# Loads in eight-token rows turned by TensorE, an instruction order from a replay of the queues, and a choice of engine for each step, in an attention-plus-MLP kernel

## The chip, the cores and the metric

The kernel runs on one core of one Trainium2 chip. The metric is the device time of one execution in microseconds (us); lower is better. Each execution also has a span, from the first to the last instruction that the profiler counts; in this case the time is 1.7 to 1.9 us longer than the span in every execution. Engines are named as in the profile: PE is TensorE (matmuls), PEld its weight loads, DVE VectorE, ACT ScalarE, POOL GpSimd, SP SyncE.

## The reference

A recurrent attention over 4 batches x 8 heads x 768 tokens x 48 channels, and then a two-layer MLP on the 3072 tokens:

```python
for t in range(S):                       # per batch and head, state is 48 x 48
    cur = outer(u * k[t], v[t])
    y[t] = r[t] @ (state + cur)
    state = w[:, None] * state + outer(k[t], v[t])
x = y with heads side by side            # (3072, 384)
h = x @ w_in                             # 384 -> 2048
g = maximum(0.01 * h, h)
out = g @ w_out                          # 2048 -> 384, fp32
```

## The kernel before

Both kernels cut the 3072 tokens into 24 stages of 128 tokens (six per batch). A stage goes through: load r, k, v; scale r and k by powers of w out of tables (`kq`); transpose (`kt`); scores (PE), causal mask (`at`, DVE); y (PE) plus the bonus term `bv`; a state update (PE, `s`); transpose of y into `xT`; first layer (PE, eviction, leaky ReLU into the ring `gring`); second layer (PE), eviction `o`, store. Every one of these is recorded as an operation of a plan, a list scheduler simulates the engines and fixes the order of each engine's instructions, and the program is emitted in that order. An engine thus waits for its next instruction in the fixed order, even where a later one could run.

Loads are issued per stage, one row of 48 fp32 (192 B) per token and head, 1024 rows in each load:

```python
def go_rk():
    ins = []
    for xi, src in enumerate((r, k)):
        a = src[b].rearrange("h t d -> t h d")[c * L:c * L + L, :, :]
        ins.append(SP.dma_start(vr.t[:, xi, :, :], a))
    return ins
# ... order of the first loads and weight pieces; "@k" style gates make one wait for another's landing
DMA_SEQ = "st0 wc st1 u wi0@rk0 wi1@rk0 st2@v1 wo0@rk2 st3@v2 wo1@v2 st4@rk3"
```

Each step belongs to one engine. The leaky ReLU is ScalarE's: it evicts the PSUM bank once as it is, and in some groups a second time with the factor 0.01 (otherwise DVE multiplies in SBUF); DVE takes the maximum:

```python
e1 = op("ACT", 0.52, (lambda ev=ev: ev(False)), ..., reads=[bk], writes=[gv...])
if two:
    hparts.append(op("ACT", 0.52, (lambda ev=ev: ev(True)), ..., reads=[bk], writes=[hv]))
# ...
m = op("DVE", 1.22 if nu == 4 else 0.69, V.tensor_tensor(..., ALU.max), ...)
```

The second number of `op` is the duration that the scheduler reckons with; in `schedule` a transfer starts when the one before is through (`x0 = max(o.end + 0.6, dma_free)`) and lands 1.4 us after its last byte.

Of the kernel before, what the change touches and what calls it, by code (L numbers as in the profile page):

```python
# [24 lines left out]
GROUPS = [1, 1] + [2] * 11  # L25
NRAW, NKQ, NKT, NVB, NAT, NPU, NB, NBV, NY, NOUT, NSS, NG = 5, 3, 3, 5, 2, 2, 3, 3, 3, 4, 2, 16
NBANK = 5
NH = 3
OB_DVE = 20
TWO = [1, 1, 1, 1] + [1, 1, 0, 0] * 4 + [0, 0, 0, 0]  # L30
MOE_BANKS = 3
QKT_DMA_FROM = 8
YT_DMA_FROM = 99
LEAD = 3.0
PERIOD = 6.0
WARM_UNTIL = 14.0
WI, WO = [4, 12], [8, 8]
DMA_SEQ = "st0 wc st1 u wi0@rk0 wi1@rk0 st2@v1 wo0@rk2 st3@v2 wo1@v2 st4@rk3"
BONUS_DVE = 0
BONUS_PE = 2  # L40
MASK_SPLIT = 2
XT_DVE = 0
S_ACT = 0
KT_SPLIT = 2
CROSS = 0.07
SAME = 0.06


class Op:
    __slots__ = ("eng", "dur", "fn", "deps", "prio", "name", "vals", "new", "xfer", "sem",  # L50
                 "start", "end", "done", "pos", "ndma", "left", "users", "snap", "mark", "waits", "semval", "slots", "count", "behind")

    def __init__(self, eng, dur, fn, name, prio):
        self.eng, self.dur, self.fn, self.name, self.prio = eng, dur, fn, name, prio
        self.deps, self.vals, self.new = set(), [], []
        self.xfer, self.sem, self.ndma = None, None, 1
        self.start = self.end = self.done = None
        self.users = []
        self.mark = False
        self.count = 1  # L60


class Val:
    __slots__ = ("pool", "name", "writers", "readers", "slot", "prev")

    def __init__(self, pool, name):
        self.pool, self.name = pool, name
        self.writers, self.readers = [], []
        self.slot = None
        self.prev = ()  # L70
# [6 lines left out]
class Pool:  # L77
    def __init__(self, name, bufs):
        self.name, self.bufs = name, bufs
        self.cur = [None] * len(bufs)  # L80
        self.until = [0.0] * len(bufs)


class Plan:

    def __init__(self):
        self.ops = []

    def op(self, eng, dur, fn, name, prio, reads=(), writes=(), after=(), xfer=None, sem=None, ndma=1,
           behind=(), joins=()):  # L90
        o = Op(eng, dur, fn, name, prio)
        o.xfer, o.sem, o.ndma = xfer, sem, ndma
        for v in reads:
            assert v.writers, (name, v.name)
            for p in v.writers:
                o.deps.add(p)
            v.readers.append(o)
        for v in writes:
            if v.writers:
                for p in v.writers:  # L100
                    o.deps.add(p)
            else:
                o.new.append(v)
            v.writers.append(o)
        for p in after:
            o.deps.add(p)
        o.deps.discard(o)
        o.behind = set(behind)
        for v in joins:
            o.behind.add(v.writers[0])  # L110
            v.writers.append(o)
            o.vals.append(v)
        self.ops.append(o)
        return o

    def schedule(self, filler=None, filler_dep=None, filler_until=0.0):
        engs = ["PE", "DVE", "ACT", "POOL", "SP"]
        free = {e: 0.8 for e in engs}
        dma_free = 0.0
        for o in self.ops:  # L120
            o.left = len(o.deps | o.behind)
            for d in o.deps | o.behind:
                d.users.append(o)
        cand = {e: [o for o in self.ops if o.eng == e and o.left == 0] for e in engs}
        order = {e: [] for e in engs}
        moe_open = 0
        ndone = 0

        def slot_for(v):
            best = None  # L130
            p = v.pool
            for i, c in enumerate(p.cur):
                if c is None:
                    t, dd = p.until[i], ()
                else:
                    us = c.readers + c.writers
                    if any(u.start is None for u in us):
                        continue
                    t, dd = max(u.done for u in us), us
                if best is None or t < best[0]:  # L140
                    best = (t, i, dd)
            return best

        def lat(d, o):
            if d.xfer is not None:
                return d.done
            if d.eng == o.eng:
                return d.end if d.eng == "PE" else d.end + SAME
            return d.end + CROSS

        while ndone < len(self.ops):
            pick = None
            for e in engs:
                best = None
                for o in cand[e]:
                    if o.name[0] == "moe" and o.new and o.name[1] >= MOE_BANKS:
                        pass
                    st = free[e]
                    for d in o.deps:
                        x = lat(d, o)  # L160
                        if x > st:
                            st = x
                    for v in o.vals:
                        for d in v.prev:
                            st = max(st, lat(d, o))
                    ok = True
                    sl = []
                    for v in o.new:
                        if v.pool is None:
                            continue  # L170
                        if getattr(v.pool, "limit", None) is not None and v.name[0] == "m":
                            open_m = sum(1 for c in v.pool.cur if c is not None and c.name[0] == "m"
                                         and any(u.start is None for u in c.readers + c.writers))
                            if open_m >= v.pool.limit:
                                ok = False
                                break
                        b = slot_for(v)
                        if b is None:
                            ok = False
                            break  # L180
                        sl.append((v, b))
                        if b[0] + CROSS > st:
                            st = b[0] + CROSS
                    if not ok:
                        continue
                    key = (max(st, free[e] + 0.02), o.prio)
                    if best is None or key < best[0]:
                        best = (key, o, st, sl)
                if best is None:
                    continue  # L190
                if pick is None or best[2] < pick[2]:
                    pick = best
            assert pick is not None, ("stuck", {e: [(o.name) for o in cand[e]][:8] for e in engs})
            _, o, st, sl = pick
            e = o.eng
            if e == "PE" and filler is not None and st < filler_until + 10:
                free[e] = max(free[e], filler_dep.end + CROSS)
                while free[e] < filler_until:
                    fd = 0.22 if free[e] < 6.8 else 0.11
# [3 lines left out]
                    f.start = free[e]  # L203
                    f.end = f.done = free[e] + fd
# [4 lines left out]
            o.start, o.end = st, st + o.dur  # L209
            o.done = o.end  # L210
            free[e] = o.end
            if o.xfer is not None:
                x0 = max(o.end + 0.6, dma_free)
                dma_free = x0 + o.xfer
                o.done = dma_free + 1.4
            o.slots = []
            for v, (t, i, dd) in sl:
                for u in dd:
                    o.deps.add(u)
                v.slot = i  # L220
                v.pool.cur[i] = v
                v.prev = tuple(dd)
# [3 lines left out]
            cand[e].remove(o)  # L226
            for u in o.users:
                u.left -= 1
                if u.left == 0:
                    cand[u.eng].append(u)  # L230
            ndone += 1
        return order

    def sync(self, order):
        for e, lst in order.items():
# [4 lines left out]
        for e, lst in order.items():  # L240
            for o in lst:
                if o.xfer is not None:
                    cnt[o.sem] = cnt.get(o.sem, 0) + 16 * o.ndma
                    o.semval = cnt[o.sem]
        known = {e: {} for e in order}
        for o in seq:
            e = o.eng
            kn = known[e]
            need = {}
            for d in o.deps:  # L250
                if d.xfer is not None:
                    key, val = ("D", d.sem), d.semval
                else:
                    if d.eng == e and e == "PE":
                        continue
                    key, val = ("E", d.eng), d.pos
                if kn.get(key, -1) >= val:
                    continue
                if key not in need or need[key][0] < val:
                    need[key] = (val, d)  # L260
            keep = []
            items = sorted(need.items(), key=lambda kv: -kv[1][1].done)
            for key, (val, d) in items:
                if kn.get(key, -1) >= val:
                    continue
                keep.append(d)
                d.mark = True
                kn[key] = max(kn.get(key, -1), val)
# [3 lines left out]
            o.waits = keep  # L272
            o.snap = dict(kn)
        for e, lst in order.items():
# [609 lines left out]
```

## Time and profile before

| kernel before | value |
|---|---|
| time, 3 runs | 197.82 us median (197.74 to 199.0) |
| profiled execution | 200.67 us, span 198.9 us |
| mean granted TensorE clock in it | 0.949 |

The page's first part gives, for each engine, busy us (share of the span) and the number of instructions:

```profile
PE 175.0 (88%) x1753; PEld 127.3 (64%) x1753; DVE 133.3 (67%) x179; ACT 116.0 (58%) x226; POOL 83.5 (42%) x82
```

The costliest groups (line, engine, operation, output<-inputs, shapes, count | busy us, mean ns | idle time of the engine just before them, and what ended it):

```profile
L636 PE MATMUL ps_g<-xT,win 128*128 128x256 bf16 (+1 forms) x624 | 75.9, 274 | 1.3 <-ACT xT L616 1.3
L711 PE MATMUL ps_g<-wout,gring 128*128 128x384 bf16 x384 | 68.5, 331 | 3.5 <-DVE gring L691 3.2
```

L636 and L711 are the two dense layers, 144 us of PE's 175. The list of waits (who waited for what: us in total, times, longest) shows the hole of the head as PE and DVE saw it:

```profile
PE ps_g L484 <- DVE kq L457: 9.6, 2, 7.9
...
DVE kq L457 <- DMA raw<-in_k_dram: 7.9, 1, 7.9
```

One wait of 7.9 us of DVE for a k load (the second line) became one wait of 7.9 us of PE for DVE (the longest of the first).

### The profile page before, as it was taken

To read this page: it belongs to the slowest core of one execution; us is meant where nothing else is said; L and a number is where in the kernel's file an instruction comes from. 1 tells how busy PE (TensorE), PEld (TensorE's weight loads), DVE (VectorE), ACT (ScalarE), POOL (GpSimd) and SP (SyncE) were. 2 spreads that over 40 slices of the span, in tenths; PEclk is the share of its full clock that TensorE was granted. 3 is DMA by queue.
4 is the path that set the end of the run, shared out by engine and by line. 5 is a ranking of instruction groups with operands and counts; after the bars stand their busy time and mean duration, and the time that the engine had idled before them with its cause. 6 is when DMAs were issued, how large, how long until landed. Compare 5 with 4: busy or idle time off the path is not lost.

```text
span 198.9 us, 4292 instructions
## 1 busy us (share of the span) xinstructions
PE 175.0 (88%) x1753; PEld 127.3 (64%) x1753; DVE 133.3 (67%) x179; ACT 116.0 (58%) x226; POOL 83.5 (42%) x82
## 2 busy tenths in 40 slices
PE   7640989488998998999998999999999999999983
PEld 5430779245865765776866757667677676676751
DVE  2521605876999999899796784975975538364531
ACT  3800648413985794657794657946679555346430
POOL 2310350435699999967867455541331100000000
PEclk9995557879999999999999999999999999999999
DMA  5799699699998589998999867982334220110112
GB/s 110 110 205 208 122 140 184 115 215 243 212 202 164 134 168 179 223 175 170 241 179 227 166 135 166 146 167 82 53 92 96 52 79 3 39 45 0 42 40 81
DMA packets 99253, 26.91 MB, mean 135 GB/s; under 512 B 93088, under 2 KB 98848, under 8 KB 99232
## 3 DMA queue, kind: packets, MB, share of 16 engines
q1 hardware_dynamic: 92896, 18.75, 52.3%
q0 software_dynamic: 2880, 3.15, 9.6%
q10 hardware_dynamic: 3456, 4.72, 6.8%
q8 instruction: 14, 0.23, 0.5%
q14 instruction: 7, 0.06, 0.1%
HBM read 20.84 MB, written 4.72 MB: 128 GB/s over the span
## 4 chain that ended last, share of the span: by engine, by line
PE 58%; DVE 22%; ACT 7%; DMA 6%; SPq 3%; issue 2%; ACTq 0%; DVEq 0%
PE ps_g L711 26%; PE ps_g L636 22%; DVE gring L691 7%; DMA raw<-in_k_dram 6%; ACT gring L669 4%; DVE kq L457 4%; DVE at L552 3%; PE ps_xy L535 3%; DVE y L575 2%; PE ps_g L613 2%; PE ps_g L484 1%; PE ps_g L568 1%; ACT h L668 1%; PE ps_g L564 1%; DVE h L687 1%
## 5 line engine op out<-in xcount | busy, mean ns | idle before, releaser
L636 PE MATMUL ps_g<-xT,win 128*128 128x256 bf16 (+1 forms) x624 | 75.9, 274 | 1.3 <-ACT xT L616 1.3
L711 PE MATMUL ps_g<-wout,gring 128*128 128x384 bf16 x384 | 68.5, 331 | 3.5 <-DVE gring L691 3.2
L669 ACT ACTIVATE gring<-ps_g 128x512 bf16<-128x512 f32 x96 | 57.8, 606 | 21.9 <-PE ps_g L636 15.4
L636 PEld LDWEIGHTS ps_g<-xT,win 128*128 128x128 bf16 x624 | 56.8, 103 | 9.1 <-ACT xT L616 2.1
L711 PEld LDWEIGHTS ps_g<-wout,gring 128*128 128x128 bf16 x384 | 36.4, 99 | 28.6 <-DVE gring L691 5.6
L523 POOL TENSOR_TENSOR bv<-vb,b 128x384 bf16<-128x384 bf16 x22 | 25.0, 1135 | 46.2 <-DVE y L575 28.8
L691 DVE TENSOR_TENSOR gring<-gring,h 128x2048 bf16<-128x2048 bf16 (+1 forms) x26 | 32.5, 1253 | 11.0 <-ACT h L668 9.4
L552 DVE TENSOR_TENSOR at<-ps_xy,tri 128x1024 bf16<-128x1024 f32 x22 | 26.8, 1217 | 15.6 <-PE ps_xy L535 15.6
L457 DVE TENSOR_TENSOR kq<-raw,tab 128x768 bf16<-128x768 f32 x24 | 27.0, 1127 | 12.3 <-DMA raw<-in_k_dram 7.9
L467 POOL TENSOR_TENSOR pu<-raw,ubc 128x384 f32<-128x384 f32 x22 | 26.5, 1205 | 8.0 <-DMA raw<-in_k_dram 8.0
L668 ACT ACTIVATE h<-ps_g 128x512 bf16<-128x512 f32 x48 | 28.6, 614 | 1.1 <-PE ps_g L636 0.9
L469 POOL TENSOR_TENSOR pr<-pu,raw 128x384 f32<-128x384 f32 x22 | 27.2, 1235 | 1.3
L722 ACT ACTIVATE o<-ps_g 128x384 f32<-128x384 f32 x22 | 10.8, 490 | 25.9 <-PE ps_g L711 25.9
L461 ACT ACTIVATE vb<-raw 128x384 bf16<-128x384 f32 x24 | 12.8, 534 | 16.2 <-DMA raw<-in_v_dram 9.8
L616 ACT ACTIVATE xT<-ps_g 128x384 bf16<-128x384 bf16 x24 | 12.0, 498 | 9.0 <-PE ps_g L613 8.8
L687 DVE TENSOR_SCALAR h<-gring 128x2048 bf16<-128x2048 bf16 x12 | 9.1, 757 | 10.3 <-ACT gring L669 10.3
L575 DVE TENSOR_TENSOR y<-ps_g,bv 128x384 bf16<-128x384 f32 x24 | 13.2, 551 | 1.6 <-PE ps_g L568 1.4
L484 PE MATMUL ps_g<-idn,kq 128*128 128x128 bf16 x64 | 5.3, 231 | 9.6 <-DVE kq L457 9.6
L471 DVE TENSOR_REDUCE b<-pr 128x8 f32<-128x384 f32 x22 | 11.9, 541 | 2.6 <-POOL pr L469 1.4
L484 PEld LDWEIGHTS ps_g<-idn,kq 128*128 128x128 bf16 x64 | 4.2, 103 | 10.3 <-DVE kq L457 10.2
L535 PE MATMUL ps_xy<-kt 48*128 48x128 bf16 x192 | 9.7, 222 | 1.1 <-DVE kt L491 0.8
L613 PE MATMUL ps_g<-idn,y 128*128 128x128 bf16 x72 | 8.5, 231 | 2.4 <-DVE y L575 2.4
(51 smaller groups left out, 104.3 us busy)
## 6 DMA issues: line engine op xcount, KB each, us to landing
raw<-in_r_dram SPq DMA_DIRECT2D x24, 192.0 KB, 3.6
raw<-in_k_dram SPq DMA_DIRECT2D x24, 192.0 KB, 3.8
raw<-in_v_dram SPq DMA_DIRECT2D x24, 192.0 KB, 3.9
out_dram<-o ACTq DMA_DIRECT2D x24, 192.0 KB, 1.9
wout<-in_moe_w_out_dram POOLq DMA_DIRECT2D x2, 768.0 KB, 11.1
win<-in_moe_w_in_dram POOLq DMA_DIRECT2D x1, 1152.0 KB, 11.4
win<-in_moe_w_in_dram POOLq DMA_DIRECT2D x1, 384.0 KB, 6.0
kt<-kq SPq DMA_TRANSPOSE x16, 3.5
```

What stands on the lines that cost most here:

```text
L457: o = op("DVE", 0.96, lambda: V.tensor_tensor(kq.t[:, :, 0:D], vr.t[:, 0:2, :, :].rearrange("p a h d -> p (a h) d"), tab[l][:, :, :, :].re ...
L467: op(bn, bd_, lambda: be.tensor_tensor(pu.t[:, :, :], vr.t[:, 1, :, :], ubc[:, :, :], ALU.mult), f"pu{n}", pr_a(n, 0.2), reads=[vr, f_u], ...
L469: op(bn, bd_, lambda: be.tensor_tensor(pr.t[:, :, :], pu.t[:, :, :], vr.t[:, 0, :, :], ALU.mult), f"pr{n}", pr_a(n, 0.3), reads=[vr, pu], ...
L523: op("POOL", 0.95, lambda: G.tensor_tensor(bv.t[:, :].rearrange("p (h d) -> p h d", d=D), vb.t[:, :].rearrange("p (h d) -> p h d", d=D), b ...
L535: o = PE.matmul(xy.t[:, 512 * s + 128 * i:512 * s + 128 * i + 128], kt.t[rows, HP + i, :], kt.t[rows, i, :], start=(i == 0), stop=True, sk ...
L552: op("DVE", 1.23, lambda: V.tensor_tensor(at.t[:, :, :], xy.t[:, :].rearrange("p (h t) -> p h t", t=128), tri[:, :].unsqueeze(1).to_broadc ...
L575: op("DVE", 0.57, lambda: V.tensor_tensor(ys.t[:, :], y.t[:, 0:DM], bv.t[:, :], ALU.add), f"ys{n}", pr_a(n, 0.5), reads=[y, bv], writes=[ys])
L636: o = PE.matmul(bk.t[:, 128 * T * f:128 * T * (f + 1)], win[:, s, 128 * fb:128 * fb + 128], xT[:, s, L * n0:L * n0 + L * T], start=(s == 0 ...
L668: return A.activation(o_ap, i_ap, AF.Copy, scale=LRELU_SLOPE)
L669: return A.activation(o_ap, i_ap, AF.Copy)
L691: (lambda j0=j0, j=j, hv=hv, flat=flat: V.tensor_tensor(flat(dst(j0, j + 1)), flat(dst(j0, j + 1)), flat(hdst(hv, 0, nu)), ALU.max)),
L711: o = PE.matmul(bk.t[:, 0:DM], gring[:, n % NG, fb, :], wout[:, fb, :], start=(fb == 0), stop=(fb == NFB - 1))
```

## The change

The intent is to feed PE earlier and to keep it fed. Its parts:

1. **Wide rows.** r and k of the first six stages and v of the first five are loaded as 128 rows of 1536 B (eight tokens of one head), so that one transfer has 128 rows in place of 1024. The tokens then lie along the row, and PE turns them with 16 small matmuls against columns of the identity.
2. **y turned by DMA** from stage 10 on, in place of PE transposes and evictions.
3. **Alternatives.** An operation may name a second and third engine with its duration there, and the scheduler takes whichever lets it start first.
4. **Replay.** After scheduling, the order is replayed against a model of the DMA queues. The landing times that come out are used for a second and a third plan, and the best of the three is kept.
5. **Sizes.** Weight pieces 4, 4, 8 each, a new order of the first loads with gates, single-stage groups at both ends, the last tile's second layer in three column thirds, four banks for the MLP, a `gring` of 12 stages instead of 16.

The diff, cut to its core:

```diff
-GROUPS = [1, 1] + [2] * 11
+GROUPS = [1, 1, 1, 1, 2, 2, 2, 2, 2, 2, 2, 2, 2, 1, 1]
-MOE_BANKS = 3
-QKT_DMA_FROM = 8
-YT_DMA_FROM = 99
-LEAD = 3.0
+MOE_BANKS = 4
+QKT_DMA_FROM = 9
+YT_DMA_FROM = 10
+LEAD = 5.5
-WARM_UNTIL = 14.0
-WI, WO = [4, 12], [8, 8]
-DMA_SEQ = "st0 wc st1 u wi0@rk0 wi1@rk0 st2@v1 wo0@rk2 st3@v2 wo1@v2 st4@rk3"
+WARM_UNTIL = 20.0
+WI = [4, 4, 8]
+WO = [4, 4, 8]
+DMA_SEQ = 'st0 st1 wi0@k1 wi1@wi0 st2@k0 uw@v0 w@r0 st3@v0 wi2@v3 u@r0 wo0@v2 wo1@v0 wo2 st4@v0 st5@v0 st6@v4'
+NWIDE = 6
+V_WIDE = 5
+GS_POOL = 8
+LAST_SPLIT = 3
+PASSES = 3
...
+                wide = n < NWIDE and (xi < 2 or n < V_WIDE)
+                    if wide:
+                        a = dram(src, (b * H * S + c * L) * D, [[8 * D, 16], [S * D, H], [1, 8 * D]])
+                        return [SP.dma_start(vr.t[:, xi, :, :].rearrange("p h d -> p (h d)"), a)]
...
+        def turn(ps, part):
+            for j in range(8):
+                for s in range(2):
+                    o = PE.matmul(ps[64 * s:64 * s + D, 64 * j:64 * j + 64], part(j), idn[:, s:128:2],
+                                  start=(j == 0), stop=True, skip_group_check=True)
...
+            elif kind == "uw":           # w and u as 4 rows, 1.5 KB together, turned by PE at once
+                def go_wu():
+                    return [A.dma_start(wu[:, 0, :, 0:D], dram(w, 0, [[2 * D, HP], [D, 2], [1, D]])),
+                            A.dma_start(wu[:, 1, :, 0:D], dram(u, 0, [[2 * D, HP], [D, 2], [1, D]]))]
+                op("ACT", 1.55, go_wu, "wu", -186, writes=[f_wu], after=gates, ...)
...
+                parts.append(op("ACT", 0.6, (lambda ev=ev: ev("ACT")), f"ga_{n0}_{j}", pr + 0.05, reads=[bk],
+                                alt=("DVE", 0.69, ...) if n0 >= GA_ALT else None, **kw))
...
+                    op("DVE", 0.79 if nu == 4 else 0.46, (lambda sc=sc: sc("DVE")), f"gs_{n0}_{j}", pr + 0.07,
+                       after=parts[-nu:], writes=[hv],
+                       alt=[("ACT", 1.92 if nu == 4 else 1.06, ...)]
+                       + ([("POOL", 2.6 if nu == 4 else 1.4, ...)] if n0 < GS_POOL else []))
...
+    landing, best = {}, None
+    for _ in range(PASSES):
+        P, order = build(landing)
+        landing, made = P.execute(order)
+        made += sum(P.execute(order, case)[1] for case in CASES)
+        made /= 1 + len(CASES)
+        if best is None or made < best[0]:
+            best = (made, P, order)
```

## The prediction

> **What bounds the kernel now.** I read the page first, then the chain of waits in order of time, then busy time by windows, then the groups by line. The busy tenths, in 40 slices of 5 us each:
>
> ```profile
> PE   7640989488998998999998999999999999999983
> DVE  2521605876999999899796784975975538364531
> PEclk9995557879999999999999999999999999999999
> DMA  5799699699998589998999867982334220110112
> ```
>
> The reader is to see two regimes. From about 50 us on, TensorE (PE) is busy nine tenths or more at full clock: there the kernel is bound by the matmuls of the two dense layers. Before that, PE has holes, and its clock is at half in slices 4 to 6. The windows (core, PE busy, PEld, DVE, ACT, POOL, granted clock, DMA share, GB/s) put the hole in place:
>
> ```profile
> 12.00:14.00 2.00, 0.02 (x1) 0.00 (x0) 0.00 (x0) 0.00 (x0) 0.00 (x0) 1.00 1.09 208
> 16.00:18.00 2.00, 0.00 (x0) 0.00 (x0) 0.00 (x0) 0.00 (x0) 0.00 (x0) 0.50 1.06 202
> 28.00:30.00 2.00, 2.00 (x22) 2.00 (x20) 0.00 (x0) 1.80 (x4) 0.00 (x0) 0.50 1.27 184
> 36.00:38.00 2.00, 1.20 (x16) 0.68 (x16) 2.00 (x4) 0.00 (x0) 1.21 (x1) 1.00 0.94 169
> 60.00:80.00 20.00, 17.85 (x187) 12.74 (x187) 19.86 (x24) 13.39 (x28) 19.59 (x16) 1.00 0.78 160
> ```
>
> From 12 to 18 us no engine works and DMA is full: everything waits for data. At 28 us PE is busy but at half clock. At 36 us VectorE (DVE) has no idle time while PE has; from 60 to 80 us DVE is busy 19.86 of 20 us. The chain says which data:
>
> ```profile
> 6.97 11.94 DMA raw<-in_k_dram
> 18.93 0.97 DVE kq L457
> ...
> 26.23 6.90 PE ps_g L636 x72
> ...
> 195.99 0.56 DVE o L722
> ```
>
> The k rows of the second stage took 11.94 us to land, behind both pieces of the first weight matrix. DVE stands in program order before that data, so even the first stage's output waits until 19.81 us. Dense work starts in earnest at 26.23 us.
>
> So the span of 198.9 us is a sum: 26.2 us of head, 169.7 us from there to PE's last matmul at 195.97, 2.9 us of last eviction and store. In the middle part, slow clock from 26.2 to 31.5 and from 39.5 to 42 us costs (5.3 + 2.5)/2 = 3.9 us, idle PE some 8.7 us (summed from the windows), and the rest, about 157 us, is matmul work.
>
> **What the Trainium skill says.**
> "TensorE: Matmul & The Clock Gate", section "Why this matters for your kernels": avoid PE gaps over about 3 us between bursts, or the clock falls back to half. The trace agrees: PE stops near 12 us, the clock averages 0.72 in 14:16 and 0.50 in 16:18. It also shows 0.70 in 38:40 after four microseconds in which PE was about half busy with no gap that long.
> "DMA: Bandwidth & Descriptors", section "Specifications": transfers need at least 512 B to reach line rate. The trace agrees: q1, nearly all 192-byte rows, holds the 16 engines 52.3% of the span for 92,896 packets, 0.523 x 198.9 x 16 / 92,896 = 17.9 ns each, 10.7 B/ns; the output's q10 (3456 packets, 4.72 MB, 6.8%) takes 62.6 ns for 1365 B, 21.8 B/ns.
> "SBUF — State Buffer", in its list of what contends: a DVE instruction with two SBUF inputs excludes a GpSimd one that reads SBUF. The trace fits: kq takes 941 ns at least and 1751 at most, GpSimd's pr 993 to 1859.
>
> **The change part by part.**
>
> *Wide rows.* Seventeen loads (r, k of six stages, v of five) become 128 rows of 1536 B instead of 1024 of 192 B. DMA time of one: before 64 packets per engine x 17.9 = 1.15 us; after 8 x 62.6 = 0.50 us. Over 17 that is 11 us of full-rate DMA off the head, and the first weight piece is held until the second stage's k has landed. SP issues a load in 0.4 to 0.6 us, so that k is issued by about 3.5 us and lands near 6 (a load takes 3.6 to 3.8 us unloaded before). The hole from 11 to 19.8 us goes. Price: turning. Each of 17 tiles needs 16 small matmuls; eight of 48 columns took 0.20 us warm (25 ns each), so I take 28 ns: 7.6 us. Eleven turns back of four transposes at 0.056 (eight took 0.45): 2.5 us. The old transposes of stages 0 to 5 go: 6 x 0.45 = 2.7 us. Each turn also needs an eviction of 0.6 to 0.7 us on DVE or ScalarE.
>
> *y turned by DMA from stage 10 on.* 14 sets of three PE transposes go (14 x 0.27 = 3.8 us of PE), and 14 evictions of 0.50 on ScalarE.
>
> *Engines per step.* Counting the built orders and multiplying by the group means: DVE goes from 133 us to about 146, as it takes 15 of the 96 first evictions (0.69 each, 10.4), 9 output copies, and fewer scalings; ScalarE goes from 116 to roughly 115 to 125, since the second eviction with a factor (48 x 0.61 = 29) becomes a scaling out of SBUF. Neither exceeds PE.
>
> *Groups and the last tile.* Single-stage groups at both ends, and the last tile in thirds. Before, the tail shows 0.50 us of PE wait before the last 2.77 us, then 2.9 us. Thirds shorten the last copy from 0.56 to about 0.25; 48 matmuls of 128 columns at 0.057 cost 2.7 against 2.6. A gain of about 0.3 us.
>
> PE sum before, warm: dense 24 x (4 x 0.66 + 2.60) = 125.8; scores 24 x 0.33 = 7.9; y 24 x 0.20 + 20 x 0.25 = 9.8; states 6.3; y turns 24 x 0.27 = 6.5; transposes 8 x 0.45 = 3.6; total 159.9. After: 125.8 + 7.9 + 9.8 + 6.3 + 10 x 0.27 + 3 x 0.45 + 7.6 + 2.5 + 0.5 = 164.5. **PE gets 4.6 us more work, not less**; the gain is that work starts earlier.
>
> Where in time? In the built order of the changed kernel PE has done about 25 us of this before its first matmul of the second layer, and 139.6 us remain (all but 10 of 96 first-layer groups, all second-layer ones, stages 6 to 23). When does it reach that point? DVE must by then have done 31.7 us by group means less 2.3 us of constants that wait for no data; the means overstate by 7% (same count for the whole kernel before: 143 against 133 busy), so 27.5 us, starting near 3.5 us: not before 31 us. In a chain of PE turn, eviction, mask, product, DVE will not be full; at 85% it is 36 us. A second estimate by DMA: the weights held 16 engines 9.6% of the span, 19.1 us; six stages wide 17 x 0.50 + 1.15 = 9.7; tables 1 to 2; a start near 3 us: all weights in by 34 us if DMA never rests, and the gated queue will rest some. **I take 36 us** for that point.
>
> From there: 139.6 x 1.01 = 141 us (the same counting on the kernel before, from its first long second-layer block at 39.5 us, gives 147.8 of work, and 147.8 + 1.2 cold + 5.7 idle falls 1.8 us short of 195.97, hence 1%). Idle: before it was 4.0 us from 60 to 196; DVE is now more loaded (about 102 us beside PE's 112 until attention ends), the replayed order and a fourth bank work against that; I take 4 us. End 2.7. Sum 36 + 141 + 4 + 2.7 = 183.7 of span; the median is 197.82 where this span is 198.9, factor 0.995: 182.7, say **183 us**.
>
> **The rivals.**
> *DVE becomes the bound.* For: 146 us of work in 183, full from 60 to 80 us already before; a PE bank held by a late eviction stops PE. Against: the last attention is spread later in the new order. It would cost 4 to 8 us more: 187 to 191.
> *Weights late or PE cold.* The weights now follow each other through gates on one queue; if the last piece lands near 42 instead of 36 us, or if a half-busy PE loses its clock between 8 and 30 us as it did at 39 us, the dense part starts 3 to 6 us later: 186 to 189.
> *The gain is smaller because the hole was hidden.* If the middle were bound by DVE or DMA rates rather than by when PE starts, an earlier start would only become idle time later: 190 or more, within 2% above 193.9. Against: from 80 to 180 us PE is over 95% busy at full clock, so a shift of the start shifts the end.
> *Better than thought.* Replay leaves PE idle under 2 us after 33 us: 178.
>
> **Range and chances.** The sum's loose terms are the 36 us point (32 to 42) and idle (2 to 8); together 177.5 to 190. Slower than 2% would need all of the 15 us eaten: 1%. Within 2% needs two rivals at once: 5%. Faster by over 2%: 94%.
>
> **What would show it.** In the changed profile: no window under 20 us without work; the second stage's k landed by 7 us; first-layer matmuls from 16 to 20 us; the first second-layer matmul at 34 to 40 us; clock 1.0 after 15 us; PE from then to its end at 95% or more, for 141 us plus idle; DVE busy 142 to 150 us; the last eviction near 0.25 us. It is wrong if the first second-layer matmul comes after 43 us, if PE idles over 8 us after it, or if PE's clock shows 0.5 in several slices.

## The result

| kernel | times of the executions, us | median | clock of the executions |
|---|---|---|---|
| before | 199.0, 197.82, 197.74, 199.0 | 198.41 | 0.949 in the profiled one |
| changed | 185.95, 186.94, 186.91, 186.15 | 186.53 | 0.981, 0.982, 0.972, 0.981 |

The ratio is 0.940, with a 95% interval of 0.935 to 0.945. It is the mean time of one kernel's fast runs over the mean of the other's fast runs in the same rounds, so it is not quite the ratio of the medians. The profiled execution of the changed kernel is the one of 185.95 us, span 184.2 us. First its page, by engine, then the busy tenths in 40 slices (of 4.6 us each now):

```profile
PE 173.1 (94%) x2108; PEld 135.1 (73%) x2108; DVE 150.2 (82%) x218; ACT 113.6 (62%) x186; POOL 88.3 (48%) x89
...
PE   7749998979999999899999999999999999999994
DVE  4956799885699995997799967996995978787792
PEclk9995799999999999999999999999999999999999
DMA  4899799999870099694979999939999732120202
```

PE has almost as many busy us as before (173.1 against 175.0) in a shorter span. DVE has 17 us more. The row of PEclk has one dip left, of two slices, where it had five slices below 0.8. The windows that answer to those shown of before (us, then PE, PEld, DVE, ACT and POOL busy, granted clock, DMA share, GB/s):

```profile
12.00:14.00 2.00, 0.00 (x0) 0.00 (x0) 0.00 (x0) 0.00 (x0) 1.89 (x2) 0.88 1.17 271
14.00:16.00 2.00, 1.74 (x24) 1.47 (x25) 1.01 (x5) 0.00 (x0) 0.00 (x0) 0.50 1.06 257
16.00:18.00 2.00, 2.00 (x24) 1.75 (x22) 1.61 (x2) 1.29 (x5) 0.00 (x0) 0.50 1.09 289
28.00:30.00 2.00, 2.00 (x55) 1.85 (x56) 2.00 (x2) 1.79 (x6) 1.32 (x2) 1.00 1.12 207
36.00:38.00 2.00, 1.71 (x34) 1.50 (x34) 0.51 (x2) 1.99 (x5) 1.98 (x2) 1.00 1.08 203
60.00:80.00 20.00, 19.23 (x192) 14.58 (x190) 17.79 (x22) 16.95 (x26) 15.70 (x12) 1.00 0.75 140
```

Two things are to be seen. From 60 to 80 us PE is now busy 19.23 of 20 us (before 17.85) and DVE has room. From 12 to 14 us PE, DVE and ACT stand still again, and the clock is at half for the 6 us that follow. A third thing needs a longer window: from 22 to 36 us DVE has no idle time at all (13.96 of 14 us busy), while PE is busy 13.26. The list of waits says what ended that stop, and the chain of waits (start us, us, what) carries it to the dense part:

```profile
PE ps_g L591 <- DMA wu<-in_u_dram: 3.0, 1, 3.0
```

```profile
8.04 6.17 DMA wu<-in_u_dram
...
34.83 2.79 POOL h L1035
...
38.93 1.22 DVE at L908
...
177.84 3.99 PE ps_g L1069 x56
181.85 0.29 DVE o L1081
```

The new stop is a wait for two loads of 1.5 KB each (the comment in the code counts them as one): the rows of w and of u that PE turns into columns. The plan gates them behind the first stage's v. The load of u is issued at 8.04 us and lands 6.17 us later, and PE stands before it in its fixed order. The window from the first matmul of the second layer's first block to PE's last (span us, PE busy, clock, DMA share, GB/s):

```profile
40.74:181.85 141.11, 140.16 (x1470) 1.00 0.67 138
```

In these 141.1 us PE is idle for less than 1 us. The kernel before, from its first long second-layer block at 39.50 us to its last matmul at 195.97, took 156.5 us, of which 150.8 were busy and 5.6 idle. So the 14.7 us of span split as follows: 10.7 us less PE time after the point where the dense part begins, 4.7 us less idle time after it, 0.6 us less tail, minus 1.2 us because that point comes later, at 40.7 instead of 39.5.

### The profile page after: what moved, and what is told of

It is laid out like the page before. It is cut to its first block, busy times and chain, and to the rows that moved or that the text cites. A ratio compares the mean times of both kernels' runs of the same rounds, so it can differ in the third digit from the quotient of the medians.

```text
span 184.2 us, 5027 instructions
## 1 busy us (share of the span) xinstructions
PE 173.1 (94%) x2108; PEld 135.1 (73%) x2108; DVE 150.2 (82%) x218; ACT 113.6 (62%) x186; POOL 88.3 (48%) x89
## 4 chain that ended last, share of the span: by engine, by line
PE 58%; POOL 13%; ACT 8%; DVE 7%; issue 7%; DMA 5%; ACTq 0%; POOLq 0%
PE ps_g L1007 24%; PE ps_g L1069 23%; POOL pu L872 5%; POOL bv L878 4%; DMA wu<-in_u_dram 3%; POOL pr L874 3%; PE ps_xy L890 3%; DVE at L908 3%; ACT h L1036 2%; ACT gring L1021 2%; PE ps_g L920 2%; PE ps_g L924 2%; DMA lnp<-in_w_dram 2%; POOL h L1035 2%; DVE gring L1042 1%
## 5 line engine op out<-in xcount | busy, mean ns | idle before, releaser
L1069 PE MATMUL ps_g<-wout,gring 128*128 128x384 bf16 (+1 forms) x416 | 69.9, 314 | 0.0
L1007 PEld LDWEIGHTS ps_g<-xT,win 128*128 128x128 bf16 x720 | 63.0, 114 | 4.3 <-issue 1.0
L1021 ACT ACTIVATE gring<-ps_g 128x512 bf16<-128x512 f32 x81 | 45.8, 600 | 19.5 <-PE ps_g L1007 18.7
L1042 DVE TENSOR_TENSOR gring<-gring,h 128x2048 bf16<-128x2048 bf16 (+1 forms) x30 | 34.3, 1147 | 8.2 <-ACT h L1036 6.6
L1036 ACT ACTIVATE h<-gring 128x2048 bf16<-128x2048 bf16 (+1 forms) x21 | 32.3, 1545 | 9.9 <-DVE gring L1021 9.4
L878 POOL TENSOR_TENSOR bv<-vb,b 128x384 bf16<-128x384 bf16 x18 | 19.5, 1088 | 34.4 <-DVE b L876 31.1
L1021 DVE CAST gring<-ps_g 128x512 bf16<-128x512 f32 x15 | 10.1, 692 | 1.9 <-PE ps_g L1007 1.6
L1081 DVE COPY o<-ps_g 128x384 f32<-128x384 f32 (+1 forms) x12 | 5.8, 486 | 4.8 <-PE ps_g L1069 4.8
L890 PEld LDWEIGHTS ps_xy<-kt 48*128 48x128 bf16 x192 | 5.5, 95 | 5.2 <-issue 2.8
L924 PE MATMUL ps_g<-vb,at 128*128 128x48 bf16 x192 | 9.0, 186 | 0.0
L920 PE MATMUL ps_g<-s,kt 128*128 128x96 bf16 x80 | 6.9, 211 | 1.9 <-DVE at L908 1.7
```

Of the source, the lines that this page charges most:

```text
L878: op("POOL", 1.1, lambda: G.tensor_tensor(bv.t[:, :].rearrange("p (h d) -> p h d", d=D), vb.t[:, :].rearrange("p (h d) -> p h d", d=D), bb ...
L890: o = PE.matmul(xy.t[:, 512 * s + 128 * i:512 * s + 128 * i + 128], kt.t[rows, HP + i, :], kt.t[rows, i, :], start=(i == 0), stop=True, sk ...
L1007: o = PE.matmul(bk.t[:, 128 * T * f:128 * T * (f + 1)], w_in_block(s, j * per + f), xT[:, s, L * n0:L * n0 + L * T], start=(s == 0), stop= ...
L1021: return A.activation(o_ap, i_ap, AF.Copy) if e == "ACT" else V.tensor_copy(o_ap, i_ap)
L1036: return A.activation(o_ap, i_ap, AF.Copy, scale=LRELU_SLOPE)
L1042: return V.tensor_tensor(flat(dst(j0, j + 1)), flat(dst(j0, j + 1)), h_ap, ALU.max)
```

## The experiments

All runs gave the correct result. The kernel before was run beside them, between 197.5 and 201.9 us. "The first second-layer matmul" is dated from the chain or from that line's instructions; "the dense part" is the time from there to PE's last matmul. Experiments that change constants let the planner make a new order, so they change more than the one thing; those marked "order kept" edit the finished order and change nothing else.

### The changed kernel again

No edit. It tells how much executions of one program differ, and serves beside the others.

> The changed kernel once more, unedited, as the measure for the others of this call: 185.5 to 187.5 us, and the same hole in the profile: TensorE idle from about 12 to 14.3 us for the small load of w and u columns, half clock from there to about 20 us, first second-layer matmul near 40.7 us.

Measured: 182.88, 185.7, 186.08 and 187.35 us at clocks 0.991, 0.991, 0.972 and 0.972. A run over 1.5% above the fastest of its kernel counts as slow, so three of these carry that label and no ratio is given; with all eight executions of this kernel the mean is 186.0 us (185.5 for these four alone). In the profiled one (182.88) the small load landed at about 11.7 us instead of 14.2, and the stop is shorter:

```profile
PE ps_g L591 <- DMA wu<-in_u_dram: 1.3, 1, 1.3
```

Its first second-layer matmul comes at 37.5 us and its last matmul ends at 178.77: again 141.3 us. The same program, 3.2 us earlier at the start of the dense part and 3.1 us shorter in span. So the head alone sets the difference, and the head differs with the landing of one small load and with the clock.

### The small load early (order kept)

```diff
     _, P, order = best
+    wu_op = [o for o in order["ACT"] if o.name == "wu"][0]
+    wu_op.deps = {d for d in wu_op.deps if d.pk is None}      # no gate
+    wu_op.start = max(d.start for d in wu_op.deps) + 0.001
+    order["ACT"].remove(wu_op)
+    order["ACT"].insert(1, wu_op)                             # second on its queue
```

> Only the place of the two small loads of w and u columns changes: issued second on ScalarE's queue, without the gate; every other engine's order is the same. Theory (the point of the first second-layer matmul came 4.7 us late because of this load: 2.25 us of stop, then some 6 us at half clock, then the second weight piece issued behind work that waits for it): no stop at 12 us, no half clock from 14 to 20, first second-layer matmul at 36 to 38 us, time 182 to 183.5 us. Rival A (VectorE sets the head: busy 18.15 of 20 us between 20 and 40): first second-layer matmul only 1 to 2 us earlier, time 185 to 186. Rival B (the last weight piece, landing near 41 us, sets it): the first second-layer matmul comes earlier but TensorE then waits before the matmuls that need the last piece, time 184.5 to 186.

Measured: 183.04, 185.11, 185.38, 184.31 us, median 184.71, ratio to before 0.931 (0.923 to 0.938). Windows of this kernel:

```profile
12.00:14.00 2.00, 2.00 (x39) 1.34 (x36) 2.00 (x6) 1.25 (x5) 2.00 (x2) 1.00 1.18 278
14.00:16.00 2.00, 1.55 (x47) 1.22 (x46) 1.83 (x4) 2.00 (x8) 1.71 (x3) 1.00 1.02 278
```

and the end of its head and of its chain:

```profile
31.94 2.79 POOL h L1035
...
37.85 0.65 PE ps_g L1069 x4
...
174.93 4.00 PE ps_g L1069 x56
178.95 0.29 DVE o L1081
```

The stop is gone and PE is busy from 12 to 14 us at full clock. The dense part starts at 37.85 instead of 40.74 us and lasts 141.1 us, to the tenth what it lasted in the changed kernel. So against the first profile of the changed kernel the small load and the half clock after it cost 2.9 us. Against its repeat they cost nothing: there PE waited 1.3 us for the load and the dense part still began at 37.5 us. Where PE waited 4.2 and 4.4 us (the profiles of the last tile whole and of y turned by PE, with the same gate) it began at 42.05 and 42.51 us. In the means the gain is less than the theory had: 1.0 us against the four executions of the same rounds (184.46 against 185.5), 1.5 against all eight, and the two sets overlap. The load lands at a different time in every profiled execution with this gate (11.7, 14.2, 15.4 and 15.7 us), and three of these four executions still have two or three half-clock windows (stretches of some 3.4 us at half clock, counted from the span and the mean clock as in the last section); that this is why the mean gains less is likely, but the unprofiled executions don't show it.

### y turned by PE throughout

```diff
-YT_DMA_FROM = 10
+YT_DMA_FROM = 99
```

> Turning of y kept on TensorE in all stages; order replanned. Theory (after about 41 us TensorE's work alone sets the end): 14 sets of 0.27 us come back, 3.8 us, time 189 to 191 us. Rival (TensorE has slack, VectorE or ScalarE bound): within 1 us of the changed kernel, or more than 6 us slower through ScalarE's 14 evictions.

Measured: 191.55, 189.02, 189.61, 190.09 us, median 189.85, ratio 0.959 (0.951 to 0.967).

```profile
42.51 0.65 PE ps_g L1069 x4
...
184.39 2.87 PE ps_g L1069 x48
```

```profile
PE ps_g L1069 <- DVE gring L1042: 1.4, 1, 1.4
```

The dense part takes 187.26 - 42.51 = 144.75 us, some 3.7 us more than 141.1. Fourteen sets of transposes at 0.27 us would be 3.8 us, but the agreement is in part chance: in that window PE is busy 142.21 us, only 2.05 more than the 140.16 of the changed kernel, and idle 1.6 us more. Of the idle time 1.4 us is one wait for the leaky ReLU before the last block, which the changed kernel doesn't have. So more PE work lengthens that part, but not one for one as I had it; whether the wait comes from the transposes or only from the new order isn't shown. (The 1.8 us by which the profiled execution starts later is its small load, for which PE waited 4.4 us.)

### Narrow loads

```diff
-DMA_SEQ = 'st0 st1 wi0@k1 wi1@wi0 st2@k0 uw@v0 w@r0 st3@v0 wi2@v3 u@r0 wo0@v2 wo1@v0 wo2 st4@v0 st5@v0 st6@v4'
-NWIDE = 6
+DMA_SEQ = 'w st0 uw@v0 st1 wi0@k1 wi1@wi0 st2@k0 st3@v0 wi2@v3 u@r0 wo0@v2 wo1@v0 wo2 st4@v0 st5@v0 st6@v4'
+NWIDE = 0
```

> Wide rows undone (no stage loaded in eight-token rows, w's table first in the queue), all else of the change kept. Theory (the gain comes from an earlier dense part that the wide rows allow): most of the gain is lost, first second-layer matmul back to 45 us or later in terms of work left, time 192 to 198 us although TensorE has about 7 us less to do. Rival (the new order and engine choice carry the gain, the rows do not matter): 184 to 189 us.

Measured: 197.48, 197.82, 196.79, 198.4 us, ratio 0.998 (0.990 to 1.005): the whole gain is gone. From its waits and its chain:

```profile
ACT vb L810 <- DMA raw<-in_v_dram: 12.3, 3, 10.0
...
PE ps_st L943 <- ACT vb L810: 10.0, 1, 10.0
```

```profile
18.12 19.80 DMA raw<-in_v_dram
...
46.13 0.65 PE ps_g L1069 x4
```

One narrow load of 192 KB, beside the weight pieces, took 19.80 us to land and held PE for 10 us. The Trainium skill, "DMA: Bandwidth & Descriptors", section "Queues, rings and completion order", says that each DMA engine takes turns between the queue rows it has work for, a packet at a time. A load of 1024 small pieces beside large weight rows would then need several turns on each engine. The two long landings fit that picture (19.80 us here and 11.94 us in the kernel before, against medians of 3.6 to 3.9 us), but no run counts the turns, so this cause is argued and not shown.

### Narrow loads in another order

```diff
-DMA_SEQ = 'st0 st1 wi0@k1 wi1@wi0 st2@k0 uw@v0 w@r0 st3@v0 wi2@v3 u@r0 wo0@v2 wo1@v0 wo2 st4@v0 st5@v0 st6@v4'
-NWIDE = 6
+DMA_SEQ = 'w st0 uw@r0 st1 u wi0@k0 wi1@k0 wi2@k0 st2@v1 wo0@k2 wo1@k2 wo2@k2 st3@v2 st4@k3'
+NWIDE = 0
```

> Narrow rows again as in e4, but the loads of stages and weights ordered as in the kernel before, so that the weights do not stand in front of stages 3 and 4 as they did in e4 (a load there took 19.8 us). Theory (narrow rows cannot be fed beside the weights whatever the order; the wide rows carry the gain): first second-layer matmul at 43 us or later, time 191 to 198. Rival (e4 only showed a bad order of loads; narrow rows with a fit order keep most of the gain): 185 to 190.

Measured: 197.23 and 198.75 us, ratio 0.999 (0.989 to 1.009). Here the weights come early and the first second-layer matmul is at 26.8 us, and it does not help:

```profile
60.00:80.00 20.00, 17.13 (x177) 13.11 (x178) 19.80 (x23) 10.25 (x19) 19.86 (x13) 0.91 0.49 106
80.00:100.00 20.00, 16.49 (x176) 13.13 (x174) 15.86 (x19) 12.14 (x20) 19.63 (x13) 1.00 0.73 156
```

PE starves from 60 to 100 us, while DVE and then POOL are full; its longest waits there are 3.5 us for the leaky ReLU and 2.1 us for y, both from DVE. So the date of the first matmul alone does not predict the time. That too little attention had been done by then is my reading, which no run tests. Both narrow kernels lose the whole gain, but the constants were tuned for wide rows, so the 11 to 12 us are an upper figure for what wide rows are worth, not a measurement of it.

### The last tile whole

```diff
-LAST_SPLIT = 3
+LAST_SPLIT = 1
```

> The last tile in one piece again, nothing else moved. One look: the part from the last first-layer matmul to the end of the span, which does not depend on the head. In the changed kernel the last 56 second-layer matmuls take 3.99 us and the span ends 2.4 us later. Theory: the last block takes 3.9 us and the span ends 2.7 us after it, so 0.2 to 0.3 us more in all. Rival: nothing, or a gain, because 48 narrow matmuls cost what the shorter last copy saves.

One execution, 187.76 us (state unknown, span 186.0), so only its end is read:

```profile
179.15 3.91 PE ps_g L1069 x24
183.09 0.56 DVE o L1081
```

From the start of that last block to the end of the span: 186.0 - 179.15 = 6.85 us, against 184.2 - 177.84 = 6.36 us in thirds. The thirds save some 0.5 us. The copy shrinks by 0.27 us (0.56 to 0.29), as predicted; what follows it, the last store, is 0.3 us shorter, and the narrower matmuls give 0.1 us back (3.99 for 3.91). The expectation had 0.2 to 0.3 us.

### One engine for each step

```diff
-        if alt is not None:
+        if False:
             o.alts.extend(alt if isinstance(alt, list) else [alt])
```

> The choice between engines undone: each step keeps its first engine (all turned tiles evicted by VectorE, all scalings on VectorE, all output copies and first evictions on ScalarE), order replanned. Theory: VectorE then has about 21 x 1.5 us of scalings less what they cost there (0.76 against 1.9), some 16 us more work, minus 10.4 us of first evictions, near its limit already; the head gets 12 evictions more on VectorE and starts later, TensorE waits in the middle: 189 to 195 us. Rival (engines per step hardly matter while TensorE is the bound): 186 to 188.

Measured: 197.56, 195.66, 191.74, 196.35 us; three are over 1.5% above the fastest, so no ratio is given. The one execution labelled fast, 191.74 us, is 5.7 us above the mean of the changed kernel (186.0), on another chip. The profiled execution is a slow one (197.56, clock 0.991). It shows this:

```profile
40.00:60.00 20.00, 16.39 (x226) 12.41 (x222) 19.97 (x31) 9.15 (x18) 7.61 (x8) 1.00 0.53 108
```

DVE is full (19.97 of 20 us) while ACT and POOL are under half, and PE is busy 16.39. Over the whole span DVE has 166.2 us and ACT 92.5. The first second-layer matmul is at 46.7 us. From its dense part on (46.7 us to PE's last matmul) PE is busy 138.8 us and idle 7.9. So the rival "DVE becomes the bound" is real for a plan without the choice, and the choice keeps it away. It is worth some 6 us by the one fast execution; the further 4 to 6 us of the slow ones are not explained.

### Without the replay

```diff
-PASSES = 3
+PASSES = 1
```

> One planning pass instead of three, so the order comes from assumed landing times and not from those of the replay. Theory (past the first second-layer matmul the order hardly matters since TensorE is full; only the head can lose): first second-layer matmul 0 to 4 us later, time 186 to 190. Rival (the replayed order carries much of the gain): over 191.

Measured: 189.98, 188.02, 187.94, 190.51 us, median 189.0, ratio 0.954 (0.945 to 0.964).

```profile
60.00:80.00 20.00, 18.85 (x191) 14.16 (x190) 19.92 (x23) 14.31 (x21) 14.95 (x12) 1.00 0.66 142
```

```profile
PE ps_g L1069 <- DVE gring L1042: 4.5, 6, 1.4
```

The three passes are worth some 3 us, but not where the theory put it. The first second-layer matmul is at 36.8 us, earlier than the changed kernel's; it is the dense part that takes 149.0 us instead of 141.1. Of these 7.9 us, 3.5 are work that had not been done before (PE busy 143.7 us for 140.2), and 4.3 are idle time (5.3 us for 1.0), with DVE full from 60 to 80 us and PE waiting 4.5 us for the leaky ReLU. My theory that landing times matter only in the head fell. Why the order is worse later isn't shown: the edit takes away the better landing times and also the choice of the best of three plans, and no run parts the two.

### The small load early and two scalings off GpSimd (order kept)

The chain of the changed kernel has a scaling on GpSimd of 2.79 us just before the dense part, which the plan had reckoned at 1.4. On top of the early small load:

```diff
+    for o in [x for x in order["POOL"] if x.name.startswith("gs_")]:
+        order["POOL"].remove(o)
+        at = [i for i, x in enumerate(order["DVE"]) if x.name == "gm" + o.name[2:]][0]
+        o.eng, _, o.fn = [a for a in o.alts if a[0] == "DVE"][0]
+        o.start = order["DVE"][at].start - 0.0001
+        order["DVE"].insert(at, o)
```

> The early small load of e1, and besides the two scalings that GpSimd does in the head (2.79 us each, half again to twice what the plan reckoned with) put on VectorE in place, right before the maxima that need them; nothing else moves. Theory (after the small load is out of the way, the wait of VectorE's maximum and mask for the first of these scalings, 1.5 us of VectorE and 1.2 us of TensorE in e1's profile, sets the first second-layer matmul): that matmul at 36 to 36.7 us instead of 37.7, the part after it 141 us as in all runs so far, time 0.8 to 1.5 us below e1, 183 to 184. Rival (the last piece of the second weight matrix, landing near 36.6 us, sets it anyway): the first such matmul comes earlier but TensorE waits in the next 3 us, time as e1 within 0.4 us.

Measured: 183.02, 182.99, 184.86, 183.32, 183.27, 185.04 us, median 183.3, ratio 0.928 (0.921 to 0.935). This is the fastest kernel: its mean, 183.75 us, is 1.2% below the 186.0 us of the changed kernel's eight executions (0.9% below the repeat's 185.5). Against the early small load alone (mean 184.46, ratio 0.931) the step is 0.7 us, inside both intervals. In its profile the 2.79 us are gone from the chain, but the dense part starts at 37.83 us, no earlier. That execution had half clock from about 9 to 12.5 us, and PE is then nearly full up to 37.8 us but for one stop:

```profile
28.19 1.25 issue
```

"issue" is time in which the engine waited for nothing that the profile shows. The stop lies within a group of twelve matmuls that has no wait in the program, and sits at the same instruction in the profiled repeat of the changed kernel (1.20 us), with the small load early (1.29) and in the first profile of the changed kernel (0.48). In all of them 473 recorded matmuls have run before it, and so they have before a shorter stop in the kernels without the replay (0.20 us) and in the replanned combination (0.26), where another operation stands there. So the stop belongs to a place in PE's stream of instructions and not to the work. What it waits for stays open.

### A replanned combination

```diff
-QKT_DMA_FROM = 9
-YT_DMA_FROM = 10
+QKT_DMA_FROM = 7
+YT_DMA_FROM = 7
-DMA_SEQ = '... st2@k0 uw@v0 w@r0 ...'
+DMA_SEQ = '... st2@k0 uw w@r0 ...'
-GS_POOL = 8
+GS_POOL = 0
```

> A try at a better version: small load without its gate and replanned, no scaling on GpSimd, y turned by DMA from stage 7 and q/k from stage 7 on (three sets of three transposes at 0.27 and two of eight at 0.45 less on TensorE, 1.7 us). Theory (the part after the first second-layer matmul is TensorE's work and nothing else): that part 139.5 us instead of 141.2, time 181 to 183. Rival (DMA turns so early collide with the last narrow loads and TensorE waits for them): part of 142 us or more, time 184 or more.

Measured: 189.3, 188.47, 191.83, 190.19, 188.19, 188.68 us, median 188.99, ratio 0.953 (0.946 to 0.960), so some 3 us slower than the changed kernel, although three sets of y transposes and two of q and k are taken from PE.

```profile
60.00:80.00 20.00, 16.65 (x178) 11.92 (x177) 16.68 (x22) 12.94 (x18) 13.86 (x12) 1.00 0.67 144
```

The dense part starts at 37.87 us, as early as the others, and takes 147.2 us, of which PE is busy 140.9 and idle 6.3; from 60 to 80 us it is busy only 16.65 of 20 us and no engine is full. The theory's 139.5 us failed. The rival's figures came (142 us or more, 184 us or more), but its cause is a small part: 0.8 us of PE's waits are for q and k turned by DMA, 3.3 for the leaky ReLU. The planner made a worse order out of parts that I had counted as better.

### Filler matmuls against the half clock (order kept)

The fastest kernel plus 18 filler matmuls on PE: 14 before the first turn, 4 before the first scores.

```diff
+    proto = [o for o in order["PE"] if o.name == "fill"][0]
+    for name, count in (("tw0_0", 14), ("sc0", 4)):
+        at = [i for i, x in enumerate(order["PE"]) if x.name == name][0]
+        for k in range(count):
+            order["PE"].insert(at, <copy of proto>)
```

> e9 with 18 more filler matmuls of 256 columns on TensorE, 14 before the first turn (where e9 waits 1.8 us for VectorE) and 4 before the first scores; nothing else moves. Theory (in all executions so far the time at half clock, twice the span times one minus the mean clock, is a whole number of 3.41 us, between 0 and 3 of them for the changed kernels, and each costs near 0.9 us; they come from the thin stretch of TensorE between 6 and 14 us): with the stretch filled, mean clock 1.000 in nearly every execution, spans of 180.5 to 181.5, time 182.3 to 183.2 with less spread than e9's 2.05 us. Rival A (the half clock comes whatever is done in that stretch): clocks spread as in e9, 0.972 to 0.991, and time 183 to 184. Rival B (the head is bound by VectorE, the clock only decorates it): clock 1.000 but the time unchanged within 0.3 us against e9's executions of clock 0.991.

Measured: 185.41, 184.11, 185.1, 184.07, 184.86, 183.76 us, median 184.49, ratio 0.929 (0.924 to 0.935) to the kernel before in its own rounds. The clock is cured in most (0.991, 1.0, 0.988, 0.998, 1.0, 1.0), but the ratio is that of the fastest kernel (0.928). Its mean is 0.8 us higher than that kernel's, on another chip, so the two cannot be told apart. In the profiled execution, the slowest of the six, a stop without a cause comes again, now earlier:

```profile
PE ps_g L924 <- issue: 1.3, 1, 1.3
```

It comes after the 220th matmul, where the kernel with the small load early has a stop of 0.68 us before another operation; and after 473 matmuls there is again a stop, of 0.36 us, although the fillers have moved other work to that place. I had expected each half-clock window that goes to give 0.9 us. It did not show. What the fillers cost stays open.

## Why the prediction was right or wrong

The direction and the range were right. The predicted 183 us is 3.5 us below the measured median of 186.5. By its own steps:

- **"I take 36 us for that point": wrong, measured 40.7.** This is the step that failed, and it failed twice. The share of 85% was near: with the small load early DVE is busy 29.3 of the 34.3 us from 3.5 to 37.8 us, which is 85% (87% in the repeat of the changed kernel, 80% in its first profile). But DVE's work up to there is 29.3 us and not 27.5. The group means had given 31.7 - 2.3 = 29.4; the 7% that I took off them, measured on the kernel before as a whole, made it too small. With 29.4 the step gives 3.5 + 29.4 / 0.85 = 38.1 us, and 37.5 to 37.9 is what the three executions with a short stop or none show. The other 2.9 us are the stop on the small loads of w and u with the half clock after it: they are absent in the profile with the load moved, and nearly so in the repeat, where it landed earlier. I had read the gates for the large loads only, and had not asked what PE meets first in its order. The sentence "no window under 20 us without work" was wrong for the same reason, and "clock 1.0 after 15 us" too: it was 0.50 from about 14 to 20 us. The first first-layer matmul, expected from 16 to 20 us, came at 21.1, and at 17.3 with the load early.
- **Dense part, "141 us" of work: right, and its 1% surcharge not needed.** PE was busy 140.2 us between those points, for 139.6 counted. Four profiles with the same order behind the head, but for two scalings (the changed kernel twice, the small load early, the scalings moved), all have 141.1 to 141.3 us; a fifth, with the fillers, has 142.0. The 0.27 us for a set of y transposes was too much: fourteen sets made PE busy 2.05 us longer, not 3.8.
- **Idle, "I take 4 us": too much, under 1 us.** The rival "better than thought" was right in this term.
- **Tail 2.7: measured 2.4**; last eviction 0.29 us for "near 0.25".
- **The factor 0.995 from span to time: wrong.** I divided the median time by the span of an execution that took 200.67 us. In one and the same execution the time is the span plus 1.7 to 1.9 us (1.75 in the one shown here). On the predicted span of 183.7 us that makes 185.5 us, and the measured median of 186.5 is then only 1 us off. Of the miss of 3.5 us, this step alone made 2.5; in the span itself, +4.7 at the start of the dense part, -3.9 in it and -0.3 after it nearly cancelled (184.2 for 183.7), which was luck.
- **Turning at 28 ns a matmul: too much.** A turn of 16 took 0.33 to 0.36 us warm, 22 ns each, and 0.55 at half clock. The second stage's k had landed by 7.1 us, as said.
- **DVE "about 146 us" (142 to 150): 150.2**, just outside; ScalarE 113.6, a little under its 115 to 125. Neither bounds the whole: over 20 us DVE was busy 18.15 at most. But for the 14 us from 22 to 36 it was full, beside a PE that was busy 13.26 of them.
- **Two readings of the kernel before were loose.** "Nine tenths or more" from about 50 us on is 17.85 of 20 us in the prediction's own line of 60 to 80. The 3.6 to 3.8 us of a load are medians of the whole kernel, not of an unloaded queue.
- **Rivals.** "Weights late or PE cold" came partly true, through a small constant instead of a weight piece. "DVE becomes the bound" did not come true over the whole; the profile with one engine per step, in which DVE is full from 40 to 60 us, points to the choice of engines as the reason. "The hole was hidden" is refuted by the repeat of the changed kernel: 3.2 us earlier at the start, 3.1 us earlier at the end.

Where the gain came from, as far as the runs show: of the 10.7 us by which less PE time remains at the start of the dense part, some 2 us are PE work handed to the DMA queues (y turned from stage 10 on). The rest is, by subtraction, mostly work done before that point, in the former hole and after it: 144 score matmuls (18 stages) remain instead of 168 (21 stages). Some 1.2 us of it is the half clock of the kernel before from 39.5 to 42 us. The 4.7 us less idle time afterwards hang on the order: PE is idle 1.0 us there, 5.3 without the replay, and 7.9 with one engine for each step. How much the wide rows alone are worth is not settled, as every narrow kernel here also had another order. The fourth bank, the new groups, the smaller `gring` and the new weight pieces were never run alone, so their share is not known either.

## What to carry to other kernels

Find the point from which the bounding engine runs full, count the work that remains after it, and predict the date of that point and the length of the rest separately: here the work in the rest was good to 1%, and the 3.2 us between two dates of one program showed as 3.1 us of span. For the date, walk through the bounding engine's own order and ask of each first operand, however small, when it is issued and behind what; 1.5 KB behind a gate cost up to 2.9 us, about as much as moving fourteen sets of transposes off PE gained (2.05 us of PE's time, at most 3.7 us in all). Take time and span from the same execution, and do not expect better single parts to give a better planned order: the replanned combination was 3 us slower, and so was the plan of one pass.

## What the Trainium skill lacked or had wrong

- "GPSIMD Engine Reference", section "4.1 Engine selection", calls GpSimd about two times slower than VectorE for two inputs and roughly line-rate for one. For the one-input bf16 scaling of 128x1024 the runs show 2.77 us on GpSimd, 0.43 us on DVE and 1.06 us on ACT. GpSimd is over six times slower than DVE here, though its spans in a profile are rough.
- "DMA: Bandwidth & Descriptors", section "Latency and other measured facts", puts the fixed cost of a transfer near 2 us. Beside full queues 1.5 KB took 4.5, 6.2, 7.4 and 7.6 us from issue to landing in four executions. A figure for a small load behind full queues is lacking, and so is one for many small rows beside large ones (192 KB in 192-byte rows: medians of 3.6 to 3.9 us in the kernel before, 19.8 us in the worst load of the narrow kernel).
- "TensorE: Matmul & The Clock Gate", section "Part 1: The HAM clock gate", gives a free-running window of 3413 ns. The runs agree: half-clock time, (1 - mean clock) x 2 x span, is near a whole number of such windows in almost every execution (before 2 to 6, changed 1 to 3, the fastest kernel 1 to 3; two of the six executions with fillers are not). The page says of the start alone that it varies between runs. What it lacks is that the number of half-clock windows over a whole kernel differs between executions of one program, and that their time goes with it: the kernel before had 195.8 to 196.6 us of span with two windows and 198.4 to 200.1 with five or six. (The fillers, which removed most windows, gained nothing, so how much of the time the windows cause stays open.)
- The same page's advice on gaps, cited in the prediction, speaks of some 3 us. The changed kernel's clock fell after PE had been idle for only 2.25 us, and the fastest kernel's fell near 9.4 us, while PE was working again after a gap of 1.8 us (busy 1.57 of the 3.5 us before 9.5); shorter gaps beside thin work went with a fall too.
- A figure is lacking for the stops of 0.2 to 1.35 us of PE that have no wait in the program and come after the same number of matmuls (220 in two kernels, 473 in nine profiles, 599 or 600 in seven), whatever the operation. If they are fetches of instructions, which no run tests, it belongs to "Runtime: NRT & Kernel Launch".
- The recorded clock is 1.00 in the first 6 us of every profile, while filler matmuls of 256 columns started about 213 ns apart at first (until 4.7 us in the kernel before) and some 110 ns apart later. The record doesn't show the cold start; the spacing does. It belongs to "TensorE: Matmul & The Clock Gate".
